# Every TensorE product of an agent-attention and gated-convolution kernel issued as four 32-column strips

## The chip, the cores and the metric

The kernel runs on one NeuronCore of a Trainium2 chip. The metric is the device time of one execution in microseconds: 417.98 us, the median of three runs (417.79 to 419.01). Lower is better. The engines are named as in the profile: PE is TensorE's matmul part, PEld its weight loads, DVE is VectorE, ACT is ScalarE, POOL is GpSimd, SP is SyncE, which issues nearly all DMAs.

## What is computed

Two stages for a batch of 4, with 12,800 rows of 128 channels. The first is an attention through 49 agents; the second is a convolution of 5 taps whose sigmoid gates a linear map, and an output projection:

```
def sm(a, b):
    s = scale * (a @ b.transpose(0, 2, 1)); s = s - s.max(-1, keepdims=True)
    e = np.exp(s); return e / (e.sum(-1, keepdims=True) + 1e-09)
a2k = sm(agents, k)
agent_v = a2k @ v
x = sm(q, agents) @ agent_v
...
gate_pre += conv_w[k][None, None, :] * xp[:, k:k + S, :]      # k = 0..4, xp padded in front
gate = 1.0 / (1.0 + np.exp(-gate_pre))
return (gate * (x @ w_val)) @ w_out
```

## The kernel before

**Folding.** The second stage never sees x. For each batch the 49 x 128 matrix agent_v is multiplied into w_val and into the five taps, and what remains per row are 49 softmax weights. The folded weights are split into an fp16 high part and a remainder, and both are stacked in the 128 rows of a stationary tile (`stat`), with an overhang of 95 rows in a second one. `fold_weights` (line 527) does this in five steps per batch: `normals` (535), a product with w_val (578), eight transposes of 128 x 128 fp16 (667), a transpose of the scaled output weights (705) and two more fp16 transposes (729).

**Units.** Keys, values and queries come in ten units of 1280 rows per batch. `score_matmuls` (387) computes the scores of one unit: eight fp32 products of 32 agent columns and 320 moving columns each, placed on the four 32-column strips of the array with `tile_position=(0, g * BLK)`, so that four run side by side. `key_scores` (406), `agent_values` (475) and `queries` (743) use it or follow it. `agent_values` multiplies the exponentials into the values: ten blocks of fp32 products of 129 columns, for the first batch in two strips of 64 columns, for the others in four of 32 (line 481). `key_max` (433) finds the largest score per agent with two small products: a transpose of a 128 x 2 tile (446), and a transpose of a 2 x 128 tile back (463). The query weights of the first four units are transposed on PE (`transposes`, 836, its matmuls at 856 to 861), all others by DMA.

**Chunks.** The output is made in chunks of 512 rows, 100 of them with the last cut in 384 and 128. `gates` (907) issues six fp16 products of 512 columns (five taps at line 931, the overhang at 935), `values` (951) two (958, 962), `project` (990) three (1003 to 1005), or one fp32 product (1010) for the two short chunks. All of these use the whole 128 x 128 array. Between them ACT takes the tanh (944), DVE forms h (971), ACT and POOL split h in two fp16 parts (979, 984), and ACT scales the output (1024).

**Order.** PE's order is written out by hand in a string (from 1106): `k`, `v`, `q` are units, `t` transposes, `m` and `f` the steps of `key_max` and `fold_weights`, `g`, `a`, `o` are `gates`, `values` and `project` of a chunk. A planner (`Plan`, 70) keeps this order for PE, models durations, and sorts the steps of the other engines and the DMA issues into one program. It adds 0.12 us when PE passes to a step of another key (line 156); the keys are `sc` for strips, `av`, `c` for chunks, `m` for small products and `t`.

## Time and profile before

| | |
|---|---|
| runs | 417.79, 417.98, 419.01 us |
| span of the profiled execution | 417.7 us |
| PE busy | 398.0 us (95%), 3905 matmuls and as many weight loads |
| DVE, ACT, POOL busy | 288.7, 299.7, 243.2 us |
| DMA | 127.64 MB, mean 306 GB/s |
| mean granted TensorE clock | 0.991 |

The profile shows one execution, span from the first to the last instruction; no separate time is listed for that execution, so its span stands beside the runs: it is 0.3 us below their median. A matmul's duration there reaches to the modelled end of a pipeline, so successive matmuls overlap on paper; what one costs is read from the step between starts. In a timeline row stand the start, the time to the last end, the engine, line and operation, what is written and read, the tile of the array (128*128 is the whole array, 128\*32 a strip of 32 columns), the moving operand, and the count. An fp32 product appears as two records. A line of the waits has the waiting engine and line, what ended the wait, the total in us, the times and the longest. PE's weight loads and matmuls are fetched as instructions by a DMA queue of their own, q8.

### The profile page before, as it was taken

What the parts mean: (1) busy time and instruction counts of PE and PEld (TensorE: products, weight loads), DVE (VectorE), ACT (ScalarE), POOL (GpSimd) and SP (SyncE); (2) the same over time, 40 slices, a digit from 0 to 9 for tenths busy, and PEclk for the clock granted to TensorE, in tenths of its full rate; (3) what the DMA queues carried; (4) which work ended last, traced back from release to release, by engine and by line L of the source; (5) the groups of instructions that cost most, each with busy time, mean ns of one, the idle gap of its engine ahead of it and who ended that gap; (6) DMA issues with size and microseconds to landing.
All of it is one profiled execution on the core that took longest, in us unless ns stands there. A gap on an engine that the chain in (4) does not pass through costs nothing.

```text
span 417.7 us, 10023 instructions
## 1 busy us (share of the span) xinstructions
PE 398.0 (95%) x3905; PEld 197.6 (47%) x3905; DVE 288.7 (69%) x529; ACT 299.7 (72%) x519; POOL 243.2 (58%) x301
## 2 busy tenths in 40 slices
PE   4859999999899999999999999999999999999996
PEld 1329634446545544345546544444564544444443
DVE  3967798957747765684896876895689598745222
ACT  0647457798785767778787686788869577887775
POOL 1410447864656626656378585564178869968552
PEclk9988999999999999999999999999999999999999
DMA  8999999999999999999999999999999998974733
GB/s 314 421 416 412 370 372 318 296 351 280 303 346 315 326 297 371 259 296 371 332 355 310 275 327 346 324 315 341 316 388 288 290 316 205 268 199 143 202 128 127
DMA packets 75132, 127.64 MB, mean 306 GB/s; under 512 B 50467, under 2 KB 50851, under 8 KB 75085
## 3 DMA queue, kind: packets, MB, share of 16 engines
q1 hardware_dynamic: 74940, 126.87, 96.7%
q8 instruction: 31, 0.51, 0.5%
q10 hardware_dynamic: 144, 0.13, 0.2%
q14 instruction: 17, 0.13, 0.1%
HBM read 79.25 MB, written 26.21 MB: 253 GB/s over the span
## 4 chain that ended last, share of the span: by engine, by line
PE 86%; DMA 5%; DVE 4%; ACT 2%; issue 1%; POOL 0%; SPq 0%; DVEq 0%; ACTq 0%
PE gate L931 25%; PE sc L390 19%; PE av L494 11%; PE val L958 5%; PE out L1003 5%; DMA ld<-kT 5%; PE gate L935 5%; PE val L962 5%; PE out L1004 5%; PE out L1005 5%; ACT ob L1024 1%; PE sc L858 1%; DVE wst L599 1%; DVE h L971 1%; DVE qmx L757 0%
## 5 line engine op out<-in xcount | busy, mean ns | idle before, releaser
L984 POOL TENSOR_TENSOR hl<-h,hh 128x512 f16<-128x512 f32 x99 | 117.2, 1185 | 98.5 <-ACT hh L979 97.7
L931 PE MATMUL gate<-x,stat 128*128 128x512 f16 (+1 forms) x500 | 124.2, 378 | 0.0
L971 DVE SCALAR_TENSOR_TENSOR h<-th,val 128x512 f32<-128x512 f32 x100 | 68.0, 680 | 69.3 <-PE val L962 33.2
L390 PE MATMUL sc<-ld,ag_sb 128*32 128x320 f32 x1280 | 99.8, 448 | 8.9 <-DMA ld<-qT 6.1
L944 ACT ACTIVATE th<-gate,unscale 128x512 f32<-128x512 f32 x100 | 68.5, 685 | 21.6 <-PE gate L935 20.1
L979 ACT CAST hh<-h 128x512 f16<-128x512 f32 x99 | 60.9, 616 | 25.4 <-DVE h L971 24.5
L1024 ACT ACTIVATE ob<-out,oscale 128x512 f32<-128x512 f32 x98 | 67.4, 687 | 15.0 <-PE out L1005 14.5
L931 PEld LDWEIGHTS <-stat 128*128 128x128 f16 x505 | 48.2, 98 | 60.2 <-issue 4.8
L762 POOL TENSOR_TENSOR qw<-sT,qmx 128x490 f32<-128x490 f32 x40 | 43.0, 1076 | 41.8 <-DVE qmx L757 41.6
L390 PEld LDWEIGHTS sc<-ld,ag_sb 128*32 128x32 f32 x1280 | 38.5, 112 | 56.9 <-issue 20.0
L494 PE MATMUL av<-ld,eT 128*32 128x129 f32 (+1 forms) x1400 | 50.7, 277 | 1.7 <-DVE eT L400 1.1
L494 PEld LDWEIGHTS av<-ld,eT 128*32 128x32 f32 (+1 forms) x1400 | 45.8, 115 | 10.0 <-issue 2.9
L803 POOL TENSOR_TENSOR pt<-qw,pt 128x490 f16<-128x490 f32 x40 | 44.9, 1124 | 2.7 <-ACT pt L789 2.6
L400 DVE STREAM_TRANSPOSE sT<-sc 128x640 f32<-128x640 f32 x40 | 33.6, 843 | 16.3 <-PE sc L390 15.5
L485 ACT ACTIVATE e<-ks,kbias 128x320 f32<-128x320 f32 x80 | 39.4, 553 | 5.6 <-DVE kbias L471 2.7
L400 DVE STREAM_TRANSPOSE eT<-e 128x640 f32<-128x640 f32 x40 | 33.0, 833 | 14.2 <-ACT e L485 8.6
L795 POOL TENSOR_SCALAR pt<-qw 128x160 f16<-128x160 f32 x80 | 31.9, 418 | 16.4 <-DVE qw L781 16.4
L416 ACT COPY ks<-sc 128x640 f32<-128x640 f32 x40 | 27.6, 693 | 19.2 <-PE sc L390 17.3
L958 PE MATMUL val<-x,stat 128*128 128x512 f16 x100 | 38.0, 380 | 0.9 <-DVE wo L738 0.6
L1003 PE MATMUL out<-hh,wo 128*128 128x512 f16 x98 | 37.3, 380 | 1.0 <-ACT ob L1024 0.8
L935 PE MATMUL gate<-x,stat 95*128 95x512 f16 x100 | 38.0, 380 | 0.0
L962 PE MATMUL val<-x,stat 95*128 95x512 f16 x100 | 38.0, 380 | 0.0
(132 smaller groups left out, 401.6 us busy)
## 6 DMA issues: line engine op xcount, KB each, us to landing
ld<-qT SPq DMA_DIRECT2D x40, 640.0 KB, 10.8
ld<-kT SPq DMA_DIRECT2D x40, 640.0 KB, 8.1
ld<-vP SPq DMA_DIRECT2D x39, 645.0 KB, 7.3
outT<-ob SPq DMA_DIRECT2D x48, 512.0 KB, 6.4
x<-x SPq DMA_DIRECT2D x18, 400.0 KB, 8.2
x<-x SPq DMA_DIRECT2D x18, 75.0 KB
x<-x SPq DMA_DIRECT2D x4, 200.0 KB, 5.6
outT<-ob SPq DMA_DIRECT2D x3, 256.0 KB
```

The lines of the kernel that those rows point to most:

```text
L390: nc.tensor.matmul(out=out[g * BLK : (g + 1) * BLK, j, 0:GT], lhsT=ag_sb[:, b, j * BLK : (j + 1) * BLK], rhs=src[:, g * GT : (g + 1) * GT] ...
L400: nc.vector.transpose(out=out.rearrange("p n (j i) -> p j n i", j=2), in_=in_.rearrange("p j (n i) -> p j n i", i=BLK),)
L494: nc.tensor.matmul(out=av[o + j : o + j + cols, 0 : C + 1], lhsT=et[:, n, j : j + cols], rhs=vt[:, n, :], start=(u == 0 and n < 2), stop=( ...
L931: nc.tensor.matmul(out=pg, lhsT=stat[:, k, :], rhs=x1[:, c : c + w], start=(k == 0), stop=False,)
L935: nc.tensor.matmul(out=pg, lhsT=stat[0 : TAPS * X2R, TAPS + 1, :], rhs=x2[0 : TAPS * X2R, o2 : o2 + w], start=False, stop=True,)
L944: lambda: nc.scalar.activation(out=th, in_=pg, func=AF.Tanh, scale=unscale[:, 0:1]),
L958: nc.tensor.matmul(out=pv, lhsT=stat[:, TAPS, :], rhs=x1s[(b * NCH + n0 // CH) // 5 % NX][:, PAD + o2 : PAD + o2 + w], start=True, stop=False,
L962: nc.tensor.matmul(out=pv, lhsT=stat[0 : TAPS * X2R, TAPS + 2, :], rhs=x2[0 : TAPS * X2R, o2 : o2 + w], start=False, stop=True,)
L971: lambda: nc.vector.scalar_tensor_tensor(out=h, in0=th, scalar=1.0, in1=pv, op0=ALU.add, op1=ALU.mult),
L979: "act", 0.18 + 0.43 * scale, lambda: nc.scalar.copy(out=hh, in_=h),
L984: lambda: nc.gpsimd.tensor_tensor(out=hl, in0=h, in1=hh, op=ALU.subtract),
L1024: lambda: nc.scalar.activation(out=ob[:, o : o + w], in_=po, func=AF.Copy, scale=oscale if w == CH else 1.0),
```

## The change

Every product but the transposes of line 858 is issued as four products of 32 stationary columns, each with its own strip of the array (`tile_position=(0, j)`) and its own 32 partitions of the output. New helpers:

```diff
+    def strips(fn):
+        for j in range(0, P, BLK):
+            fn(slice(j, j + BLK), (0, j))
+
+    def product(out, lhsT, rhs, start=True, stop=True):
+        def one(at, place):
+            nc.tensor.matmul(
+                out=out[at], lhsT=lhsT[:, at], rhs=rhs, start=start, stop=stop,
+                tile_position=place,
+            )
+        strips(one)
+
+    def turned(out, in_, identity):
+        def one(at, place):
+            nc.tensor.transpose(
+                out=out[at], in_=in_[:, at], identity=identity, tile_position=place
+            )
+        strips(one)
```

The chunks' products, the folds and the fold's transposes call them:

```diff
-                nc.tensor.matmul(
-                    out=pg, lhsT=stat[:, k, :], rhs=x1[:, c : c + w],
-                    start=(k == 0), stop=False,
-                )
...
+                product(pg, stat[:, k, :], x1[:, c : c + w], start=(k == 0), stop=False)
...
-            nc.tensor.matmul(out=po, lhsT=wo16[:, 0, :], rhs=hh, start=True, stop=False)
-            nc.tensor.matmul(out=po, lhsT=wo16[:, 1, :], rhs=hh, start=False, stop=False)
-            nc.tensor.matmul(out=po, lhsT=wo16[:, 0, :], rhs=hl, start=False, stop=True)
+            product(po, wo16[:, 0, :], hh, stop=False)
+            product(po, wo16[:, 1, :], hh, start=False, stop=False)
+            product(po, wo16[:, 0, :], hl, start=False)
...
-                nc.tensor.transpose(
-                    out=pw[:, i * P : (i + 1) * P], in_=wst[:, i, :], identity=ident16
-                )
+                turned(pw[:, i * P : (i + 1) * P], wst[:, i, :], ident16)
```

The two fp32 transposes of `key_max` and the one of the output weights become products with the identity. For the second one of `key_max`, `mrep` grows from 2 to 128 rows, zero but for the first two, by a memset at the start:

```diff
-    mrep = const.tile([2, G, BLK], F32, name="mrep")
+    mrep = const.tile([P, G, BLK], F32, name="mrep")
...
+    nc.vector.memset(mrep, 0.0)
...
-            lambda: nc.tensor.transpose(out=p1[0:2, 0:P], in_=m2, identity=ident),
+            lambda: nc.tensor.matmul(
+                out=p1[0:2, 0:P], lhsT=m2, rhs=ident, start=True, stop=True,
+                tile_position=(0, 0),
+            ),
...
-            lambda: nc.tensor.transpose(
-                out=p2[:, 0:2], in_=mrep.rearrange("j g a -> j (g a)"),
-                identity=ident[0:2, 0:2],
-            ),
+            lambda: product(p2[:, 0:2], mrep.rearrange("j g a -> j (g a)"), ident[:, 0:2]),
...
-            lambda: nc.tensor.transpose(out=po[:, 0:P], in_=wo, identity=ident),
+            lambda: product(po[:, 0:P], wo, ident),
```

The value products use 32-column strips in the first batch too, and the planner charges only for a passage to or from the transposes:

```diff
-        cols, key = (BLK, "sc") if b else (AP_, "av")
+        cols, key = BLK, "sc"
...
-                if key != kind:
-                    when += 0.12
+                if "t" in (key, kind) and key != kind:
+                    when += 0.1
```

## The prediction

> **What bounds the kernel now.** I read the page first, then what PE waits for, then PE's timeline stage by stage, then the instruction queue.

> ```profile
> span 417.7 us, 10023 instructions
> PE 398.0 (95%) x3905; PEld 197.6 (47%) x3905; DVE 288.7 (69%) x529; ACT 299.7 (72%) x519; POOL 243.2 (58%) x301
> ...
> q8 instruction: 31, 0.51, 0.5%
> ...
> PE 86%; DMA 5%; DVE 4%; ACT 2%; issue 1%; POOL 0%; SPq 0%; DVEq 0%; ACTq 0%
> ```

> (The q8 line gives packets, MB and share of the DMA engines.) PE is busy for 95% of the span and holds 86% of the chain. From 45 to 414 us it waits very little for the other engines:

> ```profile
> PE av L494 <- DVE eT L400: 1.1, 1, 1.1
> PE out L1003 <- ACT ob L1024: 0.8, 2, 0.6
> PE val L958 <- DVE wo L738: 0.6, 1, 0.6
> PE sc L1010 <- DVE h L971: 0.6, 1, 0.6
> PE av L494 <- issue: 0.5, 1, 0.5
> PE val L578 <- DVE avT L550: 0.5, 1, 0.5
> PE val L958 <- DVE h L971: 0.2, 1, 0.2
> ```

> That is 4.3 us in all, so what PE gains or loses behind the first 45 us goes almost whole into the time. One line among them, "issue", is time for which no engine answers; I come back to it. PE's groups by shape (busy, mean ns):

> ```profile
> L931 PE MATMUL gate<-x,stat 128*128 128x512 f16 x495 | 123.3, 379 | 0.0
> L390 PE MATMUL sc<-ld,ag_sb 128*32 128x320 f32 x1280 | 99.8, 448 | 8.9 <-DMA ld<-qT 6.1 <-DMA ld<-kT 2.1 <-ACT ks L416 0.6
> L494 PE MATMUL av<-ld,eT 128*32 128x129 f32 x1200 | 37.4, 273 | 1.7 <-DVE eT L400 1.1 <-issue 0.5
> L494 PE MATMUL av<-ld,eT 128*64 128x129 f32 x200 | 13.3, 299 | 0.0
> ```

> So strips (128\*32) and whole-array products (128\*128) share PE. Each fp32 product is recorded twice. What matters is not the mean but the step from one start to the next, which the timeline gives:

> ```profile
> 93.33 0.38 PE L1004 MATMUL out<-hh,wo 128*128 128x512 f16 x1
> 93.55 0.38 PE L1005 MATMUL out<-hl,wo 128*128 128x512 f16 x1
> 93.85 1.28 PE L390 MATMUL sc<-ld,ag_sb 128*32 128x320 f32 x16
> 94.95 1.29 PE L494 MATMUL av<-ld,eT 128*32 128x129 f32 x40
> 96.17 0.39 PE L1003 MATMUL out<-hh,wo 128*128 128x512 f16 x1
> ```

> A whole-array product steps by 0.22 (93.33 to 93.55), but 0.30 when strips follow (93.55 to 93.85). A second stretch has both a clean and a disturbed case:

> ```profile
> 194.74 0.38 PE L1005 MATMUL out<-hl,wo 128*128 128x512 f16 x1
> 195.05 2.41 PE L494 MATMUL av<-ld,eT 128*32 128x129 f32 x80
> 197.28 2.34 PE L390 MATMUL sc<-ld,ag_sb 128*32 128x320 f32 x32
> 199.43 0.61 PE L494 MATMUL av<-ld,eT 128*32 128x129 f32 x13
> 200.56 0.65 PE L494 MATMUL av<-ld,eT 128*32 128x129 f32 x16 [0.52 <-issue]
> ```

> Eight rounds of four score strips between strips take 2.15 (197.28 to 199.43), 0.269 a round. Twenty rounds of value strips take 2.23, 0.11 a round, four loads and four matmuls in it.

> **Part 1, the divisions that go away.** Entering strips costs 0.09 (0.30 or 0.31 instead of 0.22). The way out, and the slower first round, follow from:

> ```profile
> 248.23 1.24 PE L931 MATMUL gate<-x,stat 128*128 128x512 f16 x5
> 249.31 0.38 PE L935 MATMUL gate<-x,stat 95*128 95x512 f16 x1
> 249.63 3.44 PE L390 MATMUL sc<-ld,ag_sb 128*32 128x320 f32 x48
> 253.00 1.25 PE L931 MATMUL gate<-x,stat 128*128 128x512 f16 x5
> ```

> Twelve rounds at 0.269 are 3.23; the stretch from 249.63 to 253.00 takes 3.37, so 0.14 more. The value strips at 94.95 agree: ten rounds are 1.10, and 1.22 pass until 96.17. A visit to strips costs 0.09 + 0.14 = 0.23. I counted 41 visits in PE's timeline from 46.59 to 374.58, all behind the startup: 41 x 0.23 = **9.4 us saved**. No other engine's work covers a visit (PE's waits above), so the saving counts whole.

> **Part 2, the pace of an fp16 product as four strips.** The trace has no fp16 strip, so I bound it. At best it is today's 0.216 (five gates from 248.23 to 249.31, 1.08); a gain below that has no reason, since each strip still takes 512 columns. At worst it streams at the pace of the fp32 strips, 0.269 for 320 columns, that is 0.43 for 512. Which end is nearer is told by an fp32 product on the whole array:

> ```profile
> 412.26 0.86 PE L1010 MATMUL sc<-h,wo 128*128 128x384 f32 x2
> ```

> Two passes of 384 columns end 0.86 after the first start, the form's mean for one is 0.51, so they step by 0.35, which is 0.91 ns a column; the strips step by 0.84 ns a column. Hence fp32, not the strip, costs the double pace, and an fp16 strip should keep 0.216 a round: **0 us**, within 2 us either way if a round is off by 0.002 (the steps quoted scatter by 0.01), over the 1105 products. The loads do not bind: the value strips pass four loads and four matmuls in 0.11, half of 0.216.

> **Part 3, small products.** Transposes of 128 columns step by 0.056 today:

> ```profile
> 410.51 0.44 PE L931 MATMUL sc<-x,stat 128*128 128x128 f16 x5
> 410.79 0.22 PE L935 MATMUL sc<-x,stat 95*128 95x128 f16 x1
> ```

> (five in 0.28). As four strips each they cannot go faster than that, and the densest strips of the trace need 0.11 for four pairs. Of the fold's ten per batch, and the last chunk's eight, there are 48: 0 to 48 x 0.054 = 2.6 us; I take 1.6, nearer to the row of the strips. [...] The fp32 maximum, spread, fold and output-weight products (four batches) become two passes of up to four strips instead of one: 0.1 to 0.2 a batch, 0.5 in all. The three runs of transposes at line 858 stay whole-array; the one among chunks, free of a change today, now pays 0.23. The wider memset of mrep on DVE lies ahead of the first loads' landing: nothing. Sum of part 3: **+2.3 us** (0.5 to 3.5). The planner's order of the other engines can shift by some tenths; PE's own order is written out and stays.

> **Part 4, instructions.** This is the term I think decides. PE's 3905 loads and 3905 matmuls came in 31 blocks on q8: 252 instructions a block. At 199.8 PE stood still in the middle of one unit's strips (13 of 40 done), with "issue" as releaser. The instruction queue in that stretch, 197.9 to 199:

> ```profile
> q1 hardware_dynamic: 599, 0.15, 177.7%
> q8 instruction: 1, 0.02, 5.7%
> ```

> and in the stretch before it, 192 to 197.9, there is none:

> ```profile
> q1 hardware_dynamic: 1594, 2.02, 108.5%
> ```

> Counting back from the standstill, 13 + 32 + 80 matmuls with their loads are 250 instructions, and three products more make a block: PE entered it near 194.5 to 195, the next block's transfer began only at 197.9 behind the data, and the block was usable at 200.56. So a fetch took about 5.6 to 6 us from entering a block to use, and this block's work was through after about 5 (the last step before the standstill began some 0.7 before 200.56). Today that is rare, because a whole-array product is two instructions in 0.216: a block of them lasts 27 us. After the change it is eight in 0.216: a block lasts 32 x 0.216 = 6.9 us, a score stretch 8.6 (eight in 0.269), pure value strips 3.5 (eight in 0.11). The 1105 fp16 products of the chunks (eleven for each of 99 whole ones, eight for each of the two short ones) add three matmuls each, the 200 wide value records 200 and the folds some 270, about 3,780 in all: 15,400 instructions, 60 blocks.

> Where do they come late? In the first batch, the value products take

> ```profile
> 31.16 10.81 PE av L494 x160
> ```

> and double to 640 instructions: 2.5 blocks of 4.3 us against 5.6, 1.3 late each: 3.2 us, on the chain that starts all later work. In the later batches 16 of the 41 visits hold value strips. The block around one mixes up to 160 instructions of 0.0137 us with products at 0.027: 4.7 to 6 us. Late by 0 (a fetch in under 4.7) to 1.3 (a fetch in 6); I take 0.4 each, 16 x 0.4 = 6.4. Plain product stretches (6.9) just hold. **+9.6 us**, between 0 and 22 (all 60 blocks late by about 0.4).

> **Sum** on the profiled execution: 417.7 - 9.4 + 0 + 2.3 + 9.6 = 420.2; the median of the runs shown lies 0.3 above its span, so 420.5; I give **420**, with its own range 417 to 424. About 0.3%, 1.25 us, is what a measurement of this kernel can tell from no change.

> **Rivals.**

> *The fetch stays hidden.* If most fetches take under 4.7 us, only the standstill of today remains: 418.0 - 9.4 + 2.3 = **410.9**; half as late as I think gives 415 to 416. For it: 30 of 31 fetches today stop nobody. Against it: most of those had blocks of 8 us or more to hide in. It decides from the point where the fetch, from entry to use, is shorter than the 4.7 us of a dense block. [...] Chance of faster by this: 0.37.

> *Both terms meet.* The lateness is 5.9 to 8.3 us and cancels the rest: **418**. Chance 0.19.

> *The fetch is late in plain stretches too.* With the DMA rings as full as in the quoted stretch, a fetch of 7.3 us makes all 45 product blocks 0.4 late: 18 more, **430** and above. Chance 0.08.

> *fp16 strips do not overlap at full pace.* 1105 x (0.43 - 0.216) = 236 us more, **655**. Against it stands the fp32 comparison above. Chance 0.03.

> **How the numbers follow.** The forecast has 0.33, the rivals 0.37, 0.19, 0.08 and 0.03. Slower is 0.33 + 0.08 + 0.03 = 0.44, same 0.19, faster 0.37. The range reaches down to the hidden fetch (411) and up to 429, and leaves out the last two rivals and a little below.

> **What would show it.** Right: no step over 0.24 where products and strips meet; fp16 rounds of 0.216; about 60 blocks on q8; PE's "issue" waits, one of 0.5 now, become ten or more, each in the middle of a unit and ended some 2.6 us after a q8 transfer begins, most of them between 93 and 138, 195 and 232, 292 and 334, and in 31 to 45. Wrong: PE's issue time stays near 1 us (then 411), or it turns up in 340 to 410, where only products run (then 425 and more), or the step of an fp16 round is over 0.22.

## The result and the profile after

The changed kernel takes **432.3 us** (429.31 to 435.97, four runs) against 418.28 before; the ratio is 1.030 (95% interval 1.0255 to 1.0344). The changed kernel is slower, as forecast, but by 14 us and not by 2, and outside the range (411 to 429).

The slowest run (435.97) is left out of the ratio, and because the first profile fell on it the same kernel was profiled once more (`e11` below, span 429.6). Rows of both follow, beginning with the page of the first:

```profile
span 433.9 us, 17603 instructions
PE 394.2 (91%) x7684; PEld 241.6 (56%) x7684; DVE 289.1 (67%) x530; ACT 299.3 (69%) x519; POOL 241.9 (56%) x301
...
q8 instruction: 60, 0.98, 0.9%
...
PE 70%; DMA 15%; issue 4%; DVE 4%; POOL 2%; ACT 2%; SPq 1%; DVEq 0%; ACTq 0%; POOLq 0%
```

PE has fewer busy microseconds than before and a smaller share of a longer span: most of the loss is time in which PE stands still. The instruction queue brought 60 blocks where it brought 31. What PE waited for between 30 and 425 us in the second profile (total, times, longest):

```profile
PE av L518 <- issue: 9.7, 7, 2.6
PE gate L271 <- DMA x<-x: 4.3, 2, 2.2
PE av L280 <- DVE wst L615: 1.0, 1, 1.0
PE out L271 <- issue: 1.0, 1, 1.0
```

The waits on "issue" were 0.5 before and are 11 now (two smaller ones stand further down the list); and there is a wait on the x2 copies (x<-x) that the kernel before did not have. The timeline of the second profile, where products and strips meet:

```profile
257.11 1.49 PE L271 MATMUL gate<-x,stat 128*32 128x512 f16 x24
258.41 3.42 PE L414 MATMUL sc<-ld,ag_sb 128*32 128x320 f32 x48
261.64 1.48 PE L271 MATMUL gate<-x,stat 128*32 128x512 f16 x24
```

Six fp16 products take 1.30, that is 0.217 each, as on the whole array, and twelve score rounds take 3.23 (they took 3.37 before). The step of 0.31 on entry and the slower first round are gone: parts 1 and 2 did what the sum says. One standstill in detail, from the first profile:

```profile
319.09 2.37 PE L518 MATMUL av<-ld,eT 128*32 128x129 f32 x73
324.37 0.64 PE L518 MATMUL av<-ld,eT 128*32 128x129 f32 x5 [2.91 <-issue]
```

PE stops in the middle of a run of value strips. The DMA queues from 316 to 321.8, and from 321.8 to 324:

```profile
q1 hardware_dynamic: 529, 2.13, 101.4%
```

```profile
q1 hardware_dynamic: 239, 0.89, 100.7%
q8 instruction: 1, 0.02, 2.9%
```

No block started in the first stretch; the one that PE needs begins at 321.85 behind the data, and PE goes on at 324.37, 2.5 later. Counting PE's instructions (matmuls, loads and its waits for semaphores) one after the other from 1 in the second profile, its ten standstills of this kind end at numbers 961, 1217, 1729, 3265, 3521, 3777, 7105, 7361, 7617 and 11457. Each is 193 more than a multiple of 256, and each ends 2.3 to 2.7 us after a q8 transfer began: all ten stops fall at the end of a block of 256. They cost 12.5 us together (each gap less an ordinary step of 0.2).

By the same count the kernel before had two such stops, not one: at numbers 2241 and 4033, that is at 107.25 and 200.56, 1.8 us together. The first stands among its waits as one for DVE:

```profile
107.25 0.98 PE L494 MATMUL av<-ld,eT 128*32 128x129 f32 x28 [1.14 <-DVE eT L400]
```

DVE was done with eT at 106.90, and a q8 transfer had begun at 104.84, 2.4 before PE went on; so I put this stop down to the block.

What a stop can draw after it is in the busy times by stretch of the first profile (the granted clock stands after POOL's count):

```profile
320.00:323.60 3.60, 1.46 (x55) 1.19 (x43) 2.40 (x4) 1.21 (x3) 0.83 (x2) 1.00 1.03 413
323.60:327.00 3.40, 2.63 (x27) 1.89 (x31) 0.00 (x0) 1.96 (x5) 2.77 (x3) 0.50 1.02 419
327.00:330.00 3.00, 3.00 (x56) 2.64 (x52) 2.71 (x4) 1.14 (x2) 0.36 (x1) 0.99 1.17 327
```

The clock is at 0.50 from 323.62 to 327.03. PE, back at 324.37, works in 2.7 of these 3.4 us. How much slower it is at this clock, a stretch before it shows, at 0.50 from 224.63 to 231.46:

```profile
226.65 1.09 PE L271 MATMUL out<-hh,wo 128*32 128x512 f16 x8
227.50 0.67 PE L271 MATMUL out<-hl,wo 128*32 128x512 f16 x4
227.93 0.67 PE L271 MATMUL val<-x,stat 128*32 128x512 f16 x4
```

Three fp16 products take 1.28 there, 0.427 each instead of 0.217. So I put the cost of the half clock at half of PE's work in it, an estimate: another 1.3.

### The profile page after: what moved, and what is told of

It is laid out like the page before. It is cut to its first block, busy times and chain, and to the rows that moved or that the text cites. A ratio compares the mean times of both kernels' runs of the same rounds, so it can differ in the third digit from the quotient of the medians.

```text
span 433.9 us, 17603 instructions
## 1 busy us (share of the span) xinstructions
PE 394.2 (91%) x7684; PEld 241.6 (56%) x7684; DVE 289.1 (67%) x530; ACT 299.3 (69%) x519; POOL 241.9 (56%) x301
## 4 chain that ended last, share of the span: by engine, by line
PE 70%; DMA 15%; issue 4%; DVE 4%; POOL 2%; ACT 2%; SPq 1%; DVEq 0%; ACTq 0%; POOLq 0%
PE gate L271 24%; PE sc L414 14%; PE out L271 12%; PE av L518 9%; PE val L271 9%; DMA x<-x 6%; DMA ld<-kT 5%; DMA x<-pt 4%; DVE h L980 2%; POOL hl L993 1%; POOL pt L815 1%; PE sc L870 1%; PE sc L271 1%; POOL pt L807 1%; ACT ob L1033 0%
## 5 line engine op out<-in xcount | busy, mean ns | idle before, releaser
L271 PE MATMUL gate<-x,stat 128*32 128x512 f16 (+2 forms) x2400 | 153.8, 382 | 8.0 <-DMA x<-x 7.4
L271 PEld LDWEIGHTS <-stat 128*32 128x32 f16 (+1 forms) x3232 | 106.0, 97 | 81.4 <-issue 10.7
L414 PEld LDWEIGHTS sc<-ld,ag_sb 128*32 128x32 f32 x1280 | 45.5, 112 | 47.2 <-issue 11.2
L271 PE MATMUL val<-x,stat 95*32 95x512 f16 (+2 forms) x800 | 64.6, 383 | 1.1 <-DVE h L980 0.6
L271 PE MATMUL out<-hh,wo 128*32 128x512 f16 x784 | 63.6, 381 | 2.1 <-issue 1.3
L774 POOL TENSOR_TENSOR qw<-sT,qmx 128x490 f32<-128x490 f32 x40 | 41.5, 1037 | 41.9 <-DVE qmx L769 41.9
L518 PE MATMUL av<-ld,eT 128*32 128x129 f32 x1600 | 51.7, 274 | 10.9 <-issue 9.7
L518 PEld LDWEIGHTS av<-ld,eT 128*32 128x32 f32 x1600 | 46.1, 109 | 17.5 <-issue 11.9
L271 PEld LDWEIGHTS <-wo 128*32 128x32 f16 x1188 | 38.7, 97 | 30.0 <-issue 6.6
L271 PE MATMUL out<-hl,wo 128*32 128x512 f16 x392 | 41.6, 381 | 0.6 <-POOL hl L993 0.6
```

The source lines that it names most:

```text
L271: nc.tensor.matmul(out=out[at], lhsT=lhsT[:, at], rhs=rhs, start=start, stop=stop, tile_position=place,)
L414: nc.tensor.matmul(out=out[g * BLK : (g + 1) * BLK, j, 0:GT], lhsT=ag_sb[:, b, j * BLK : (j + 1) * BLK], rhs=src[:, g * GT : (g + 1) * GT] ...
L518: nc.tensor.matmul(out=av[o + j : o + j + cols, 0 : C + 1], lhsT=et[:, n, j : j + cols], rhs=vt[:, n, :], start=(u == 0 and n < 2), stop=( ...
L774: lambda: nc.gpsimd.tensor_tensor(out=d, in0=sa, in1=qmx[x].unsqueeze(2).to_broadcast([P, NBLK, A]), op=ALU.subtract,),
```

## The experiments

**The two suspects apart.** The theory is that instruction blocks reach PE late. The rival comes from the diff's last lines: with another charge the planner also orders the steps of the other engines and the DMA issues anew; two waits on x<-x point there. E1 keeps the strips and gives the planner its old charge and keys, so that DVE, ACT, POOL and the DMA queue run in the old order:

```diff
-                if "t" in (key, kind) and key != kind:
-                    when += 0.1
+                if key != kind:
+                    when += 0.12
...
-        cols, key = BLK, "sc"
+        cols, key = BLK, "sc" if b else "av"
```

> All products in strips as in the change, but the planner charges and keys its steps as before, so every other engine and the DMA queue have the order of the kernel before. Theory (instruction blocks come late for PE): the loss stays for the larger part, 422 to 429 us, with some ten PE standstills that end 2.5 us after a q8 transfer begins, about 14 us together. Rival (the new order of the DMA issues makes the x2 copies late): 411 to 414 us and no wait on x<-x.

Measured: 432.35 us (429.79 to 433.69), ratio 1.034 (1.029 to 1.039). The largest of its waits of PE, from 30 to 400 us:

```profile
PE av L518 <- issue: 9.6, 10, 2.5
PE sc L414 <- issue: 2.2, 1, 2.2
PE val L271 <- DVE h L980: 1.0, 3, 0.5
PE out L271 <- ACT ob L1033: 1.0, 2, 0.7
PE out L271 <- issue: 1.0, 1, 1.0
```

SyncE's 255 DMA issues stand in the order of the kernel before. No wait on x<-x is left, and the time is the same. Fourteen standstills at block ends cost 15.1 us, and two of them, of 2.7 and 2.8 us, are followed by 3.4 us at half clock, 3.4 us lost in sum by the same estimate. So the late blocks, without the new order, are enough for a loss of this size. The theory's range was still some 3 us too low; the half clock, which it left out, is as much.

E2 is the other half: the products of the kernel before with the new charge and keys (the same lines, the other way).

> The products of the kernel before, with the planner's charge and keys of the change, so the other engines and the DMA queue have the order of the changed kernel. Theory (instruction blocks): 418 to 422 us, at most the waits on x<-x cost some us. Rival (order): 426 us and more, with the two long waits on x<-x.

Measured: 427.89 us (424.89 to 429.9), ratio 1.022 (1.015 to 1.029). This went to the rival: the new order costs a kernel of whole-array products 10 us, though with one long wait on x<-x and not two. The largest of its waits, from 47 to 400 us:

```profile
PE gate L935 <- DMA x<-x: 4.5, 2, 3.9
PE av L494 <- DVE qr L776: 1.7, 1, 1.7
PE val L958 <- DVE h L971: 1.7, 4, 0.6
```

Among the issues, the pair of x2 copies that stood at places 131 and 132 now stands at 136 and 137, and 3.4 us at half clock follow the wait of 3.9. So both suspects cost about 10 us or more by themselves, yet the changed kernel, which has both, is no slower than E1, which has one. E11 is the changed kernel again, unaltered, to see how the two share the time.

> The changed kernel once more, to see in a second profile what its new DMA order costs when the blocks come late as well: with whole-array products that order cost 10 us, with strips nothing. Theory (PE held back by late blocks gives the late x2 copies time to land): this profile has under 3 us of waits on x<-x and 12 to 16 us of standstills on issue, 430 to 434 us. Rival (order and blocks add, and the equal medians were chance): waits on x<-x of 5 us and more, standstills under 12, again 430 to 434.

Measured: 432.47 us (429.81 to 433.8). Its waits stand above: 4.3 on x<-x, between the two expectations, and 12.5 at the block ends, where E1 had 15.1. It has one stretch at half clock behind a stop where E1 had two, and this one follows a wait on x<-x (PE goes on at 223.47, the stretch is 223.90 to 227.31). Neither expectation holds as it was put. In the changed kernel the new order costs 4.3 us of waits and 1.7 of half clock, and its blocks cost 12.5 where those of E1 cost 15.1 and 3.4: about as much less. Why they come less late is not shown.

**Double the instructions.** E3 issues every chunk product of E1 as two of 256 columns, all taps of one half and then of the other; E4 does the same to the whole-array products of the kernel before.

```diff
+            for a in range(0, w, w // n):
+                z = a + w // n
                 for k in range(TAPS):
                     c = PAD - HALO + o2 + k
-                    product(pg, stat[:, k, :], x1[:, c : c + w], start=(k == 0), stop=False)
+                    product(pg[:, a:z], stat[:, k, :], x1[:, c + a : c + z], start=(k == 0), stop=False)
```

> As the strips with the old order, but each chunk product of 512 columns is issued as two of 256, so that the chunks take twice the instructions for the same columns (about 24,000 on PE, 94 blocks). Theory: a block of chunk products then lasts 3.5 us against a fetch of 4.5 to 6, so nearly every one comes late, some 70 blocks by 1 to 2 us: 500 to 560 us. Rival (the array's pace or the order): at most 1100 x 0.004 = 4 to 5 us more than the strips with the old order.

> The kernel before with the same halves on the whole array: twice the instructions in the chunks, but a block of them still lasts 128 x 0.109 = 14 us. Theory: no late blocks but in the value strips, 420 to 425 us (1100 x 0.003 us more, and one or two more standstills). Rival (a split product itself is slow, whatever the blocks): as far above the kernel before as the halved strips are above the strips.

Measured: E3 521.64 us, E4 421.75 us, one run each. E3's queues, chain, and its largest waits:

```profile
q8 instruction: 94, 1.54, 1.2%
...
PE 74%; issue 16%; DMA 4%; DVE 2%; POOL 1%; ACT 1%; SPq 0%; DVEq 0%; POOLq 0%; ACTq 0%
```

```profile
PE gate L271 <- issue: 26.4, 18, 3.0
PE out L271 <- issue: 24.6, 15, 3.7
PE av L518 <- issue: 11.1, 5, 3.6
PE sc L414 <- issue: 9.1, 7, 3.1
```

The same columns with twice the instructions in strips cost 89 us more; the split itself costs the whole array 3.5. By the count above, E3's standstills at block ends come to 82 us. At 3.5 us a block the chunks now wait wherever they stand, while plain stretches of them did not wait at 6.9. This tells the theory from an explanation by the array's pace or by the split itself.

**Less data in the way.** E7 and E8 let each output DMA carry an eighth of its columns (so seven eighths of the output are not written), in E1 and in the kernel before.

```diff
-                out=outT[b, :, n0 + w - n : n0 + w], in_=ob[:, lo : lo + n]
+                out=outT[b, :, n0 + w - n : n0 + w - n + n // 8], in_=ob[:, lo : lo + n // 8]
```

> The strips with the old order, but each output DMA carries only the first eighth of its columns, so seven eighths of the output are left unwritten and 23 of 128 MB are not moved. Theory (an instruction block waits behind the data on the DMA engines): blocks arrive sooner, the standstills that were 15 us fall to 5 to 11: 421 to 428 us. Rival (a fetch takes the same whatever else moves): 431 to 433.

> The kernel before with the same thin output DMAs (seven eighths of the output unwritten), the control for the one above. Both theories: 416 to 418.5 us, since PE bounds it; if it falls by several us, the DMA bounds the kernel before as well.

Measured: E7 422.93 us (422.14 to 425.84), E8 418.78 (ratio to the kernel before 0.997, 0.993 to 1.0005). With 23 of 128 MB taken off the DMA engines the strips gain 9.4 us and the whole-array kernel nothing that can be told. In E7's profile (an execution of 425.84) the standstills at block ends are 10.7 us, against 15.1, and one stretch at half clock follows them, against two. So a block waits at least in part behind data: with these 23 MB gone, the standstills are 4.4 us shorter.

**Parts alone.** E5 gives the chunk products two strips of 64 columns (two instruction pairs a product instead of four), E6 leaves them on the whole array and keeps only the other strips.

```diff
+    def product2(out, lhsT, rhs, start=True, stop=True):
+        for j in range(0, P, AP_):
+            at = slice(j, j + AP_)
+            nc.tensor.matmul(
+                out=out[at], lhsT=lhsT[:, at], rhs=rhs, start=start, stop=stop,
+                tile_position=(0, j),
+            )
```

> As the strips with the old order, but each chunk product is two strips of 64 columns instead of four of 32, so the chunks take half the instructions and a block of them lasts 14 us. Theory (blocks come late, divisions cost 0.23 a visit): if 64 and 32 columns can follow each other freely, the standstills among the chunks go and the saving stays, 413 to 418 us; if going from 64 to 32 costs as from 128 to 32, steps of 0.31 show at each visit and it is 420 to 426. Rival (strips of chunks lose time whatever their count of instructions): 430 as with 32 columns.

> Only the chunk products stay on the whole array; folds, maxima, small transposes and the first batch's value products are strips, with the old order. This is part 3 of the prediction and the late blocks of the first batch alone, with the visits still paid and some 20 more of them at the folds. Theory: 418 + 2 for the small products + 3 to 4 for late blocks between 31 and 48 us + 3 to 5 for the added visits = 426 to 429. Rival (the chunks' instructions cause all of the loss): 418 to 421.

Measured: E5 426.75 us (425.64 to 427.36), ratio 1.018 (1.014 to 1.022). Its timeline, products in strips of 64 and then of 32:

```profile
97.77 0.38 PE L281 MATMUL out<-hl,wo 128*64 128x512 f16 x2
98.09 1.28 PE L422 MATMUL sc<-ld,ag_sb 128*32 128x320 f32 x16
```

The step is 0.32: passing from 64 to 32 columns costs as much as from 128 (0.31), so nothing is saved, and of its 43 blocks four still come late (5.4 us, most of it in the first batch). The second branch of the expectation held in what it says of the step; the time is 0.8 above its 426.

E6 took 424.26 us (423.48 to 424.6), ratio 1.012 (1.008 to 1.016): 2 us under the theory's range and 3 over the rival's. Its chunk 0 starts 4.1 us later than before; two standstills at 40.3 and 46.7 account for 3.2 of it, and all that comes later adds 1.0. The late blocks of the first batch are thus a loss of their own, and the added visits cost less than I had put.

E9 is E1 with the first batch's value products in two strips of 64 columns again, as before the change.

```diff
-        cols, key = BLK, "sc" if b else "av"
+        cols, key = (BLK, "sc") if b else (AP_, "av")
```

> The strips with the old order, but the first batch's value products again in two strips of 64 columns, half the instructions between 31 and 46 us. Theory: the two standstills there (1.9 and 2.1 us) go or shrink to under 0.5 each, 428 to 430 us. Rival (the first batch's late start comes from the changed maxima and folds): no change, 432.

Measured: 427.09 us (424.17 to 428.92), 5 under E1 and under the expectation. Both standstills between 31 and 46 are gone; its chunk 0 starts 2.0 us earlier than in the kernel before, where E1's starts 3.7 later. From 95 us on blocks come late as in E1, in other places.

**Strips where blocks last long.** E10 keeps the whole array except in three stretches where score strips come often and no value strips run. A flag, set at each chunk, chooses the form of every product and transpose that is added until the next:

```diff
+STRIPS = ((0, 9), (24, 36), (48, 61))
...
+        if w[0] == "g":
+            split[0] = any(lo <= w[1] < hi for lo, hi in STRIPS)
```

> Strips for chunks and small products only in three stretches where visits to score strips stand close and no value products run (chunks 0 to 8, 24 to 35, 48 to 60); all else as before, old order. Theory: some 18 visits cost nothing, no block comes late there (8.6 us a block in scores, 6.9 in chunks), so 4.1 us saved, 0.5 to 1 given back at the small products: 414 to 416, against 418 before. Rival (strips lose among the chunks too): 420 or more.

Measured: **416.26 us** (414.91 to 418.72, nine runs) against 418.91 for the kernel before beside it, ratio 0.9947 (0.9919 to 0.9975). The gain, 2.7 us, is a little smaller than expected. Its waits of PE from 47 to 400 us, and one visit without its steps:

```profile
PE out L283 <- ACT ob L1053: 1.0, 2, 0.7
PE val L283 <- DVE wo L770: 0.7, 1, 0.7
PE val L274 <- DVE avT L588: 0.5, 1, 0.5
PE sc L426 <- DMA ld<-qT: 0.3, 1, 0.3
PE val L274 <- DVE h L1000: 0.2, 1, 0.2
PE val L283 <- DVE h L1000: 0.2, 1, 0.2
```

```profile
246.10 3.42 PE L426 MATMUL sc<-ld,ag_sb 128*32 128x320 f32 x48
249.33 1.49 PE L283 MATMUL gate<-x,stat 128*32 128x512 f16 x24
```

No wait on issue is left, with 40 blocks instead of 31, and the kernel is faster than both others. Read against the profile before, PE's lag falls by 0.24 to 0.35 at each of the 17 visits in the three stretches, 4.3 us in all, as part 1 says. The profile's lead of 3.9 holds 2.3 more, at the two visits where a block came late in the kernel before and none does here; the rest goes back at small products and short waits.

## Why the prediction fell short

Slower came true, but not for the reason that carried the forecast. In the changed kernel the late blocks cost net about what part 4 put. The step that failed there is the one on the planner's order, set at some tenths; the half clock, which the sum does not have, comes behind it. With the old order (E1) it would have been part 4 that failed.

- **Part 1, 9.4 us saved: right.** The steps are gone in the timeline, and where no block comes late the strips gain on the kernel before at the rate of the sum: from 160 to 184 us, with four visits, E1's lag behind it shrinks from 7.2 to 6.2, and from 241 to 288, with six, from 9.0 to 7.6.
- **Part 2, the pace: right.** 0.217 a product; plain chunks last 2.38 to 2.39 in both kernels.
- **Part 3, 2.3 us: too high.** The fold's eight transposes in strips, in the first profile:

```profile
255.00 0.63 PE L280 MATMUL av<-ident,wst 128*32 128x128 f16 x32
255.44 0.62 PE L271 MATMUL out<-hh,wo 128*32 128x512 f16 x8
```

  They pass in 0.44, or 0.055 each, no slower than whole (0.056). I had taken the pace of the fp32 strips. Only the fp32 product of the output weights costs more, 0.22 instead of 0.10; `normals` costs less (0.23 instead of 0.39), and so does the product with w_val (0.09 instead of 0.16). Part 3 comes to about nothing.
- **Part 4, 9.6 us for late blocks: the right mechanism, made up wrongly.** 12.5 us in the changed kernel, or 10.7 more than before; 15.1 with the old order. "I take 0.4 each" for 16 visits did not hold: eight blocks behind the first batch came late, by 0.5 to 2.7 and 8.3 in all, and the two of the first batch by 4.2 and not 3.2. That the sum came near is in part luck. The time from entering a block to using the next, which I took as 4.7 to 6, is 5.4 to 7.1 at the ten; counted with PE's waits for semaphores, even the block that I read was entered at 194.3, so that its fetch took 6.2. The places were as named (31 to 48, around 105 to 117, 205 to 219, 320) but for one at 61.7, and plain product stretches held at 6.9 us a block, as E1 and E3 show from both sides. The ten blocks that stopped PE had 3.8 to 6.6 us of work.
- **Not in the sum at all: the half clock**, by estimate 1.7 us lost in the second profile and 3.4 in E1. I had priced a stop at its own length. The stretches at 0.50 measured here are 3.4 and 6.8 us long.
- **"The planner's order of the other engines can shift by some tenths": wrong, and the largest miss.** It costs 10 us with whole-array products (E2), and in the changed kernel 4.3 us of waits on x<-x (7.4 in the first profile), with 1.7 of half clock behind them. I had followed PE's order, which is fixed, and not the issues in the DMA queue, which are not: some x2 copies now stand behind transposes, loads and outputs that they stood ahead of.
- **The base, "0.3 above its span": too little.** Later executions have both numbers, and the time is 1.7 to 2.5 us above the span. So the execution profiled before took some 419.7, more than any of the runs beside it, and 420.2 of span stands for some 422 of time.

For the second profile, in spans: 417.7 - 9.4 + 0 (part 3) + 10.7 (12.5 less the 1.8 of the two late blocks before) + 4.3 + 1.7 = 425.0, against 429.6. PE's other waits behind 30 us, for DVE, ACT and POOL, are 5.1 in sum where they were 2.7, which makes 2.4 of the rest. The last 2.2 us I could not assign. One rival has a sum that does not fit: 18 us more on the forecast of 420 is 438, and 430 only on the 411 of a hidden fetch.

## What to carry to other kernels

A cheaper division of the array was paid here in instructions, 60 blocks instead of 31. Before a product is split, work out how long a block of PE's instructions will last at the new pace, and compare it with the time from entering a block to using the next, 5.4 to 7.1 us at the late blocks of the second profile. Where a block lasts longer, split; where it does not, leave the product whole. Keep the planner's order fixed while you compare, and price a stop with the half clock that can follow it (3.4 or 6.8 us at 0.50 in these runs).
